# A long convolution's filter transform: groups taken in pairs, second-stage products of 404 instead of 202 columns, and the first four folds split between VectorE and GpSimd

## Chip, cores and metric

The kernel runs on one core of a Trainium2 chip. The metric is the device time of one execution in microseconds (us), median over runs. All data are float32.

## What is computed

The reference is a gated long convolution followed by a small mixture-of-experts step. What matters here is the first part, above all the filter:

```
h_mlp  = max(pos_emb @ w1, 0) @ w2          # 12608 x 128
h_filt = h_mlp * exp(-0.01 * pos)
u      = x * v                               # 4 x 12608 x 128
y      = irfft(rfft(u, 2S) * rfft(h_filt, 2S))[:S]
out    = x * y        # then 128 rows of each batch pass through an expert network
```

The kernel replaces the long FFT by a transform of length 101 x 250, done as two matrix products (two stages). The filter is transformed once, for all 128 channels; the signal is transformed for 4 batches x 128 channels.

## The kernel before

The program has three parts on the time line. `h_hid` (L274) computes the filter in time order into the buffer `big`. `h_spec` (L354) transforms the filter and writes its spectrum to DRAM (`hd`). The loop at L1040 then takes the signal, 128 steps of four channels, through forward transform, product with the filter's spectrum and inverse transform; behind it, interleaved, come the output products and the selection for the experts. The change lies in `h_spec` alone.

`h_spec` treats the 128 channels in NG = 32 groups of four, 404 columns (4 x 101) each. Per group `g`:

- **fold** (L367 to L373): one addition and one subtraction, both with two inputs in SBUF, 101 x 504 elements each. Groups 0 to 3 are folded ahead of the loop by VectorE (L390); later ones by GpSimd, each issued by `fold(g + 4)` at the end of `fwd(g)`. There are four fold buffers (`fbo`), so the fold of `g + 4` overwrites what the first stage of `g` reads.
- **first stage** (`fwd`, L375): 16 products of 101 columns. Each float32 product has two records in the trace, so 32 at L382. An even group writes two PSUM banks (`a`), an odd group the two halves of one double bank (`c`, number 73 in the order). ScalarE copies both halves into `te` (L385); `te` has two buffers.
- **second stage** (L397 to L402): 8 products of 202 columns, two column halves `h` times two parities `e` times two row halves `w`; 16 records. They write `p` and `q`, the halves of a double PSUM bank: `c_74` for even groups, `c_72` for odd ones. They use 64 rows x 64 columns of the array, the first stage 101 rows x 63 columns.
- **combination**: ScalarE copies `q` (L404), VectorE runs four instructions (L407, L408, two at L410), all of them reading `p` in PSUM. L410 writes the buffer `ht` (two buffers), which SyncE sends to `hd` (L411).

The loop at L392 runs one group ahead in the first stage: the order on TensorE is first stage of `g + 1`, second stage of `g`, first stage of `g + 2`, second stage of `g + 1`, and so on. Engines work their instructions in program order; waits between them are put in by the framework from what each instruction reads and writes. The program order of ScalarE, VectorE and GpSimd is the order in which the lines above are written.

Of the kernel before, what the change touches and what calls it, by code (L numbers as in the profile page):

```python
# [18 lines left out]
NQ = 64  # L19
N1, N2, N3 = 101, 250, 125  # L20
# [3 lines left out]
NG = 32  # L24
# [15 lines left out]
JH = (N3 + 1) // 2  # L40
# [123 lines left out]
def hyena_moe(ctx, tc, xg, x2, pos, bw, ww, wg, mw1, mw2, fo, c1, gx, cf, ci, wm, tk, out):  # L164
    nc = tc.nc
# [9 lines left out]
    def view(t, off, shape):  # L175
        n = int(np.prod(shape[1:]))
        r = t[:shape[0], off:off + n]
        if len(shape) > 2:
            ax = "abcd"[:len(shape) - 1]
            r = r.rearrange(f"p ({' '.join(ax)}) -> p {' '.join(ax)}", **dict(zip(ax[1:], shape[2:])))  # L180
        return r

    def buf(name, k, shape):
        o, n, w = OFF[name]
        return view(arena, o + k % n * w, shape)
# [7 lines left out]
    def ps1(k, shape, name):  # L193
        return view((*bank1, *bank2[::2])[k], 0, shape)

    def ps2(k, shape, name):
        return view(bank2[k], 0, shape)
# [30 lines left out]
    fo_sb = view(arena, OFF["wx"][0] + 32 * JH, [128, 2, NQ])  # L228
# [4 lines left out]
    def rev(t):  # L233
        return t.rearrange("p (s i) -> p s i", i=N1)[:, :, ::-1]

    def nat(t):
        return t.rearrange("p (s i) -> p s i", i=N1)

    def load_u(t):
        b, g = divmod(t, NG)  # L240
        if b < B:
            for k, n in enumerate("xv"):
                nc.sync.dma_start(buf(n, t, [NP, XC]), xg[b, :, g, k])

    def stage_u(t):
        if t >= B * NG:
            return
        x, v = buf("x", t, [NP, XC]), buf("v", t, [NP, XC])
        nc.gpsimd.tensor_tensor(out=x, in0=x, in1=v, op=ALU.mult)  # L249

    def load_h(t):
        if t < B * NG:
            nc.sync.dma_start(buf("ht", t, [128, 2 * HC]), hd[:, t % NG])

    def mm2(o, lhsT, rhs, **kw):
        kw = kw or dict(start=True, stop=True)
        w = 32 if spare[0] else NQ
        for a in range(0, 128, w):
            nc.tensor.matmul(o[a:a + w], lhsT=lhsT[:, a:a + w], rhs=rhs, **kw)
# [94 lines left out]
    def h_spec():  # L354
        te = {}

        def tps(g):
            if g % 2:
                t = ps2(1, [128, 2, 512], f"htp_{g}")
                return [t[:, e, :HC] for e in range(2)]  # L360
            return [ps1(e, [128, HC], f"htp_{g}_{e}") for e in range(2)]

        def pqs(g):
            t = ps2(0 if g % 2 else 2, [128, 2, 512], f"hpq_{g}")
            return [t[:, e, :HC] for e in range(2)]

        def fold(g, eng=nc.gpsimd):  # L367
            if g >= NG:
                return
            fb[g] = view(arena, fbo[g % 4], [N1, 2, 2, 4, JH])  # L370
            hg = hb[:, :, 4 * g:4 * g + 4]
            for k, op in enumerate((ALU.add, ALU.subtract)):
                eng.tensor_tensor(out=fb[g][:, k], in0=hg[:, :, :, :JH], in1=hg[:, :, :, N3:JH - 1:-1], op=op)  # L373

        def fwd(g):  # L375
            b = fb.pop(g)
            tp = tps(g)
            t = te[g] = buf("te", g, [128, 2, HC])
            for e in range(2):
                for s in range(4):  # L380
                    for w in range(2):
                        nc.tensor.matmul(tp[e][w * NQ:w * NQ + JH, s * N1:(s + 1) * N1], lhsT=b[:, w ^ e, e, s], rhs=c1_sb[:N1, 0],  # L382
                                         start=True, stop=True)
            for e in range(2):
                nc.scalar.copy(out=t[:, e], in_=tp[e])  # L385
            fold(g + 4)

        fb = {}
        for g in range(4):
            fold(g, nc.vector)  # L390
        fwd(0)
        for g in range(NG):  # L392
            if g + 1 < NG:
                fwd(g + 1)
            p, q = pqs(g)
            t = te.pop(g)
            for h in range(2):  # L397
                c = slice(h * 2 * N1, (h + 1) * 2 * N1)
                for e in range(2):
                    for w, o in enumerate((p, q)):  # L400
                        r = slice(w * NQ, w * NQ + JH)
                        nc.tensor.matmul(o[e * NQ:(e + 1) * NQ, c], lhsT=fo_sb[r, e], rhs=t[r, e, c], start=True, stop=True)  # L402
            qs = buf("qs", g, [128, HC])
            nc.scalar.copy(out=qs, in_=q)  # L404
            vs = buf("yz", g, [128, HC])
            ht = buf("sd", g, [128, 2, HC])
            nc.vector.tensor_tensor(out=nat(vs), in0=rev(p), in1=nat(qs), op=ALU.subtract)  # L407
            nc.vector.tensor_tensor(out=nat(p), in0=nat(p), in1=rev(qs), op=ALU.add)  # L408
            for e, op in enumerate((ALU.add, ALU.subtract)):
                nc.vector.tensor_tensor(out=ht[:, e], in0=p, in1=vs, op=op)  # L410
            nc.sync.dma_start(hd[:, g], ht.rearrange("p e c -> p (e c)"))  # L411
            if NG - 5 <= g < NG - 3:
                stage_u(g - NG + 5)
                load_u(g - NG + 7)
            if g == NG - 2:
                stage_u(2)
            if g >= NG - 3:
                load_h(g - NG + 3)
# [487 lines left out]
    class Experts:  # L906
# [36 lines left out]
        def second(self, yp, hs, c0, c1):  # L943
            for c in range(c0, c1):
                mm2(yp, hs[:, c], self.m2[:, c], start=(c == 0), stop=(c == 7))
# [85 lines left out]
    for t in bank2[2:] + bank1 + bank2[:2]:  # L1031
        nc.vector.memset(t, 0.0)
    h_hid()
    h_spec()
    ex = None
    te, uv, ys, sd, ph = {}, {}, {}, {}, {}
# [3 lines left out]
    for t in range(NT + LAG):  # L1040
        g = t % NG
# [3 lines left out]
        if t < NT:  # L1045
            pq = ps2(1 - t % 2, [128, 2, 512], f"pq_{t}")
# [18 lines left out]
            o = t - 1 in uv  # L1065
# [37 lines left out]
        if i >= 0 and i % NG in LA:  # L1103
            if i % NG == LA[0]:
                ph[b] = P1(b)
            k, e = divmod(LA.index(i % NG), 2)
# [60 lines left out]
```

## Time and profile before

| | |
|---|---|
| median of 3 runs | 901.03 us (898.41 to 903.42) |
| the profiled execution | 897.32 us |
| its span, first to last instruction | 895.5 us |
| mean granted TensorE clock | 0.987 |
| busy: TensorE, VectorE, GpSimd, ScalarE | 97%, 90%, 85%, 70% of the span |
| the filter transform's stage | about 33 to 116 us of the span |

The profile counts times from the first instruction of the span. "PE" is TensorE's matrix products, "PEld" its weight loads, "DVE" VectorE, "ACT" ScalarE, "POOL" GpSimd, "SP" SyncE, whose queue issues the DMAs. Ends of matrix products are modelled in the trace, starts are recorded. The idle time in brackets is that of the engine just before the instruction, with what ended it.

### The profile page before, as it was taken

The page shows a single profiled execution, that of the slowest core. Times are in us where ns is not written, and L with a number is a line of the kernel's source. Part 1 is how long each engine was busy: PE and PEld are TensorE (multiplying, and loading weights), DVE is VectorE, ACT ScalarE, POOL GpSimd, SP SyncE. Part 2 cuts the span into 40 slices and gives each one's busy share as a digit, 9 for nine tenths or more (in the row PEclk, how much of TensorE's full clock was granted, in tenths as well). Part 3 has the DMA queues.
Part 4 walks back from the last instruction along what each step waited for, and adds up shares of the span by engine and source line. Part 5 has one row for each costly group of instructions (what it writes and reads, how often), then busy time and mean ns, then how long its engine had stood idle before and what let it go on. Part 6 is the DMA issues. An engine that isn't in the chain of part 4 may idle for free.

```text
span 895.5 us, 46412 instructions
## 1 busy us (share of the span) xinstructions
PE 865.7 (97%) x19606; PEld 763.4 (85%) x19606; DVE 807.6 (90%) x1543; ACT 627.9 (70%) x2242; POOL 763.9 (85%) x834
## 2 busy tenths in 40 slices
PE   8999989999999999999999999999999999999965
PEld 6788768999999889888899798888998898879954
DVE  8998899999999899999998898999998989997883
ACT  6655575555558988885579798855698888646920
POOL 5898659999999889898999798999998989988710
PEclk9999999999999999999999999999999999999996
DMA  7044587777887967688779766788797767855810
GB/s 251 35 174 172 205 291 226 213 217 230 262 248 246 296 219 220 200 247 250 243 234 299 224 213 207 231 247 236 250 300 237 221 199 227 253 176 179 267 60 7
DMA packets 83512, 195.06 MB, mean 218 GB/s; under 512 B 9639, under 2 KB 46608, under 8 KB 83304
## 3 DMA queue, kind: packets, MB, share of 16 engines
q1 hardware_dynamic: 83048, 191.57, 67.6%
q8 instruction: 154, 2.52, 1.1%
q0 software_dynamic: 256, 0.52, 0.2%
q14 instruction: 54, 0.44, 0.2%
HBM read 151.46 MB, written 40.60 MB: 214 GB/s over the span
## 4 chain that ended last, share of the span: by engine, by line
PE 71%; DVE 16%; ACT 5%; POOL 4%; issue 3%; DMA 2%; POOLq 0%; DVEq 0%; SPq 0%; ACTq 0%
PE c L263 19%; PE a L426 15%; PE c L268 15%; ACT arena L601 4%; PE c L546 3%; PE a L542 3%; PE a L546 3%; PE c L542 3%; PE c L402 2%; PE a L382 2%; DVE arena L440 2%; DVE c L441 2%; PE c L382 2%; DVE arena L446 1%; DVE ms L696 1%
## 5 line engine op out<-in xcount | busy, mean ns | idle before, releaser
L263 PE MATMUL c<-ci_sb,arena 128*26 128x126 f32 x8128 | 261.0, 271 | 2.1 <-POOL arena L453 1.6
L263 PEld LDWEIGHTS c<-ci_sb,arena 128*26 128x26 f32 x8128 | 244.7, 104 | 5.1 <-POOL arena L453 1.8
L268 PE MATMUL c<-arena,cf_sb 128*32 128x404 f32 x2048 | 214.0, 502 | 3.3 <-ACT arena L428 1.3
L426 PE MATMUL a<-c_sb,arena 128*32 128x202 f32 (+1 forms) x4096 | 216.1, 334 | 0.0
L426 PEld LDWEIGHTS a<-c_sb,arena 128*32 128x32 f32 (+1 forms) x4096 | 174.5, 108 | 26.7 <-issue 12.8
L249 POOL TENSOR_TENSOR arena<-arena 128x500 f32<-128x500 f32 x128 | 161.9, 1265 | 11.3 <-DMA arena<-in_xg_dram 11.3
L428 ACT COPY arena<-a 128x404 f32<-128x404 f32 x256 | 128.1, 501 | 50.2 <-PE a L426 48.8
L477 ACT COPY big<-c 128x824 f32<-128x824 f32 x127 | 106.3, 837 | 78.2 <-PE c L263 77.9
L453 POOL TENSOR_TENSOR arena<-arena 128x404 f32<-128x404 f32 x127 | 124.0, 977 | 39.0 <-DVE arena L447 30.7
L601 ACT ACTIVATE arena<-arena 128x128 f32<-128x128 f32 x502 | 147.4, 299 | 11.7 <-DVE arena L591 9.5
L268 PEld LDWEIGHTS c<-arena,cf_sb 128*32 128x32 f32 x2048 | 100.8, 109 | 35.6 <-issue 18.8
L440 DVE TENSOR_TENSOR arena<-c,arena 128x808 f32<-128x808 f32 x127 | 126.8, 998 | 3.8
L441 DVE TENSOR_TENSOR c<-c,arena 128x808 f32<-128x808 f32 x127 | 126.7, 998 | 0.0
L454 POOL TENSOR_TENSOR arena<-arena 128x404 f32<-128x404 f32 x127 | 123.6, 973 | 0.0
L601 ACT ACTIVATION_READ_ACCUMULATOR arena<-arena 128x1 f32 x502 | 96.0, 191 | 0.0
L529 POOL TENSOR_TENSOR arena<-big 128x512 f32<-128x512 f32 x72 | 89.8, 1285 | 0.7 <-PE c L542 0.4
L446 DVE TENSOR_TENSOR arena<-c,arena 128x404 f32<-128x404 f32 x127 | 73.6, 579 | 12.9
L435 DVE TENSOR_TENSOR c<-c,arena 128x404 f32<-128x404 f32 x128 | 74.6, 583 | 11.6 <-ACT arena L271 8.2
L432 DVE TENSOR_TENSOR c<-c,arena 128x404 f32<-128x404 f32 x128 | 75.0, 586 | 9.6 <-ACT c L765 4.9
L497 POOL TENSOR_TENSOR big<-big,arena 128x184 f32<-128x184 f32 x128 | 74.5, 582 | 10.0
L271 ACT COPY arena<-c 128x404 f32<-128x404 f32 x128 | 63.6, 497 | 24.2 <-PE c L268 23.1
L496 POOL TENSOR_TENSOR big<-big,arena 128x184 f32<-128x184 f32 x128 | 75.0, 586 | 1.3 <-ACT arena L478 1.3
(196 smaller groups left out, 1433.5 us busy)
## 6 DMA issues: line engine op xcount, KB each, us to landing
arena<-in_xg_dram SPq DMA_DIRECT2D x256, 250.0 KB, 3.9
arena<-hd SPq DMA_DIRECT2D x128, 404.0 KB, 4.5
out_dram<-arena SPq DMA_DIRECT2D x60, 420.0 KB, 5.4
arena<-in_x_dram SPq DMA_DIRECT2D x36, 420.0 KB, 4.7
hd<-arena SPq DMA_DIRECT2D x32, 404.0 KB, 3.0
arena<-in_x_dram SPq DMA_DIRECT2D x48, 210.0 KB, 5.0
arena<-in_pos_dram SPq DMA_DIRECT2D x15, 202.0 KB, 4.5
arena<-in_x_dram SPq DMA_DIRECT2D x4, 315.0 KB, 4.5
```

The source lines that it names most:

```text
L249: nc.gpsimd.tensor_tensor(out=x, in0=x, in1=v, op=ALU.mult)
L263: nc.tensor.matmul(o[32 * k:32 * k + c.stop - c.start], lhsT=lhsT[:, c], rhs=rhs, start=True, stop=True)
L268: nc.tensor.matmul(pq[w][a:a + 32], lhsT=cf_sb[:, 2 * w + a // NQ, a % NQ:a % NQ + 32], rhs=te[:, a // NQ], start=True, stop=True)
L426: nc.tensor.matmul(tps[s // 2][c, s % 2], lhsT=u[:, s, c], rhs=c1_sb[:, 0:k + 2:k + 1], start=True, stop=True)
L428: nc.scalar.copy(out=te[:, :, 2 * h:2 * h + 2].rearrange("p e s i -> p s e i"), in_=tps[h])
L440: nc.vector.tensor_tensor(out=mt, in0=uv, in1=ht[:, 0].unsqueeze(1).to_broadcast([128, 2, HC]), op=ALU.mult)
L441: nc.vector.tensor_tensor(out=uv, in0=uv, in1=ht[:, 1].unsqueeze(1).to_broadcast([128, 2, HC]), op=ALU.mult)
L453: eng.tensor_tensor(out=nat(sd[:, 0]), in0=nat(yz[:, 0]), in1=rev(yz[:, 1]), op=ALU.add)
L454: eng.tensor_tensor(out=nat(sd[:, 1]), in0=rev(yz[:, 0]), in1=nat(yz[:, 1]), op=ALU.subtract)
L477: nc.scalar.copy(out=ay[:, t % NG, :NJ + JM, ss], in_=o3[:, :, :NJ + JM].rearrange("p s x -> p x s"))
L529: nc.gpsimd.tensor_tensor(out=cm[:, e].rearrange("p j (g s) -> p j g s", s=4), in0=av[0], in1=av[1], op=op)
L601: nc.scalar.activation(out=x, in_=x, func=AF.Copy, accum_out=self.sc[:, j:j + 1])
```

## The change

In `h_spec` the loop now works in pairs. At each even `g` it issues the first stages of `g` and `g + 1`, then the second stages of both, now as one function `second`, with four products of 404 columns in place of eight of 202. The combinations of the two groups follow as before, one per pass. Ahead of the loop groups 0 and 1 are folded by VectorE, groups 2 and 3 by GpSimd.

```
+        def second(g):
+            pq = pqs(g)
+            t = te.pop(g)
+            for e in range(2):
+                for w, o in enumerate(pq):
+                    r = slice(w * NQ, w * NQ + JH)
+                    nc.tensor.matmul(o[e * NQ:(e + 1) * NQ], lhsT=fo_sb[r, e], rhs=t[r, e], start=True, stop=True)
+            return pq
+
         fb = {}
         for g in range(4):
-            fold(g, nc.vector)
-        fwd(0)
+            fold(g, nc.gpsimd if g > 1 else nc.vector)
         for g in range(NG):
-            if g + 1 < NG:
+            if g % 2 == 0:
+                fwd(g)
                 fwd(g + 1)
-            p, q = pqs(g)
-            t = te.pop(g)
-            for h in range(2):
-                c = slice(h * 2 * N1, (h + 1) * 2 * N1)
-                for e in range(2):
-                    for w, o in enumerate((p, q)):
-                        r = slice(w * NQ, w * NQ + JH)
-                        nc.tensor.matmul(o[e * NQ:(e + 1) * NQ, c], lhsT=fo_sb[r, e], rhs=t[r, e, c], start=True, stop=True)
+                held = [second(k) for k in (g, g + 1)]
+            p, q = held[g % 2]
             qs = buf("qs", g, [128, HC])
```

How the order moves on TensorE, at the start of the stage: the difference between the two programs (a row is a run of equal instructions; L394 is the new second stage, L402 the old one).

```order
 L382 MATMUL c_73<-c_sb,arena 63x101 x16
-L402 MATMUL c_74<-arena 64x202 x8
+L394 MATMUL c_74<-arena 64x404 x4
+L394 MATMUL c_72<-arena 64x404 x4
 L382 MATMUL a_70<-c_sb,arena 63x101 x8
 L382 MATMUL a_71<-c_sb,arena 63x101 x8
-L402 MATMUL c_72<-arena 64x202 x8
 L382 MATMUL c_73<-c_sb,arena 63x101 x16
```

Both second stages now stand together behind both first stages; in every pair two changes of shape take the place of four.

The waits that these instructions carry in the changed program, for groups 2 and 3 (a name in brackets is the engine that is waited for):

```order
L382 MATMUL c_73<-c_sb,arena 63x101 x14
L394 MATMUL c_74<-arena 64x404 [waits DVE_49,Activation_49]
L394 MATMUL c_74<-arena 64x404
L394 MATMUL c_74<-arena 64x404 [waits Activation_49]
L394 MATMUL c_74<-arena 64x404
L394 MATMUL c_72<-arena 64x404 [waits DVE_49,Activation_49]
L394 MATMUL c_72<-arena 64x404
L394 MATMUL c_72<-arena 64x404 [waits Activation_49]
```

The second stage of an odd group, in `c_72`, waits for VectorE to be done with the odd group before it, and for the copies of a first stage that ended only one second stage earlier.

ScalarE in the loop, before, and then in the changed program (L404 there is L407 here):

```order
L404 COPY arena<-c_72 128x404
L385 COPY arena<-c_73 128x404 x2
L404 COPY arena<-c_74 128x404
L385 COPY arena<-a_70 128x404
L385 COPY arena<-a_71 128x404
```

```order
L385 COPY arena<-a_70 128x404
L385 COPY arena<-a_71 128x404
L385 COPY arena<-c_73 128x404 x2
L407 COPY arena<-c_74 128x404
L407 COPY arena<-c_72 128x404
```

The two copies of `q` now come one behind the other, both behind the copies of the odd group's first stage.

GpSimd ahead of the loop, in the changed program (rows 12 and on of 781): 

```order
L347 TENSOR_TENSOR big<-big,arena 101x128x4 [waits Activation_49] x14
L373 TENSOR_TENSOR arena<-big 101x504 [waits DVE_49,PE_49,Pool_49]
L373 TENSOR_TENSOR arena<-big 101x504 [waits PE_49]
L373 TENSOR_TENSOR arena<-big 101x504 x2
L373 TENSOR_TENSOR arena<-big 101x504 [waits DVE_49,PE_49]
```

Four folds stand here ahead of the first that waits for a first stage; they wait for the filter in time order to be complete, as VectorE's first fold does.

## Rows read from the trace of the kernel before

**Rows 1.** The page: busy time of TensorE and VectorE over the span, and the clock that was granted in 40 slices of it.
```profile
PE 865.7 (97%) x19606; PEld 763.4 (85%) x19606; DVE 807.6 (90%) x1543; ACT 627.9 (70%) x2242; POOL 763.9 (85%) x834
PEclk9999999999999999999999999999999999999996
```
**Rows 2.** The chain that ended last, in order of time (start, length, what), 28 to 48 us.
```profile
35.06 1.39 PE c L382 x31
36.45 0.85 PE c L402 x16
37.29 1.54 PE a L382 x32
38.83 0.84 PE c L402 x16
39.68 1.54 PE c L382 x32
41.21 0.84 PE c L402 x16
```
**Rows 3.** The time line of TensorE (start, length, line, shape, count): the start of the stage, four stages from its middle, and its end.
```profile
33.46 0.39 PE L382 MATMUL a<-c_sb,arena 101*63 101x101 f32 x4
36.38 0.92 PE L402 MATMUL c<-arena 63*64 63x202 f32 x16
...
45.91 0.92 PE L402 MATMUL c<-arena 63*64 63x202 f32 x16
46.76 1.61 PE L382 MATMUL a<-c_sb,arena 101*63 101x101 f32 x32
48.29 0.92 PE L402 MATMUL c<-arena 63*64 63x202 f32 x16
49.14 1.61 PE L382 MATMUL c<-c_sb,arena 101*63 101x101 f32 x32
50.68 0.92 PE L402 MATMUL c<-arena 63*64 63x202 f32 x16
...
109.93 0.92 PE L402 MATMUL c<-arena 63*64 63x202 f32 x16 [1.04 <-DVE arena L410]
110.78 1.58 PE L426 MATMUL a<-c_sb,arena 128*32 128x202 f32 x32
```
**Rows 4.** The same, looked at through narrow windows: the last rounds of the second stage that began at 48.29 us, the last four rounds of the first stage that began at 49.14 us, and the eight records of 404 columns on 64 x 64 of the array at L309.
```profile
48.86 0.35 PE L402 MATMUL c<-arena 63*64 63x202 f32 x4
...
50.15 0.51 PE L382 MATMUL c<-c_sb,arena 101*63 101x101 f32 x7
50.49 0.26 PE L382 MATMUL c<-c_sb,arena 101*63 101x101 f32 x2
...
10.34 0.91 PE L309 MATMUL c<-arena 64*64 64x404 f32 x8
```
**Rows 5.** The time line of ScalarE and of VectorE around the second stage of 45.91 us.
```profile
46.08 0.89 ACT L385 COPY arena<-c 128x404 f32<-128x404 f32 x2 [1.03 <-PE c L382]
46.94 0.50 ACT L404 COPY arena<-c 128x404 f32<-128x404 f32 x1
...
43.04 0.57 DVE L407 TENSOR_TENSOR arena<-c,arena 128x404 f32<-128x404 f32 x1
45.24 0.57 DVE L407 TENSOR_TENSOR arena<-c,arena 128x404 f32<-128x404 f32 x1
46.47 1.06 DVE L410 TENSOR_TENSOR arena<-c,arena 128x404 f32<-128x404 f32 x2
47.47 0.58 DVE L407 TENSOR_TENSOR arena<-c,arena 128x404 f32<-128x404 f32 x1
```
**Rows 6.** The time line of VectorE: the end of the combination of group 29, and the waits of L410 for a transfer between 48 and 112 us.
```profile
108.72 1.06 DVE L410 TENSOR_TENSOR arena<-c,arena 128x404 f32<-128x404 f32 x2
...
54.23 1.06 DVE L410 TENSOR_TENSOR arena<-c,arena 128x404 f32<-128x404 f32 x2 [0.80 <-DMA hd<-arena]
73.25 1.07 DVE L410 TENSOR_TENSOR arena<-c,arena 128x404 f32<-128x404 f32 x2 [0.75 <-DMA hd<-arena]
85.32 1.06 DVE L410 TENSOR_TENSOR arena<-c,arena 128x404 f32<-128x404 f32 x2 [0.80 <-DMA hd<-arena]
104.31 1.06 DVE L410 TENSOR_TENSOR arena<-c,arena 128x404 f32<-128x404 f32 x2 [0.73 <-DMA hd<-arena]
```
**Rows 7.** The folds at the start: time lines of VectorE and of GpSimd in narrow windows, then groups by line, VectorE's folds that started from 32.1 to 35.2 us and GpSimd's from 39.5 to 52 us (busy time, mean ns of one, idle before).
```profile
32.13 0.68 DVE L373 TENSOR_TENSOR arena<-big 101x504 f32<-101x504 f32 x1
35.70 3.01 DVE L373 TENSOR_TENSOR arena<-big 101x504 f32<-101x504 f32 x2
37.17 1.54 DVE L373 TENSOR_TENSOR arena<-big 101x504 f32<-101x504 f32 x1
...
35.20 1.51 POOL L373 TENSOR_TENSOR arena<-big 101x504 f32<-101x504 f32 x1 [3.54 <-DVE arena L373]
36.67 2.96 POOL L373 TENSOR_TENSOR arena<-big 101x504 f32<-101x504 f32 x2
...
L373 DVE TENSOR_TENSOR arena<-big 101x504 f32<-101x504 f32 x6 | 3.7, 676 | 0.1
...
L373 POOL TENSOR_TENSOR arena<-big 101x504 f32<-101x504 f32 x14 | 14.8, 1099 | 0.0
```
**Rows 8.** The chain that ended last, in order of time, 98 to 125 us: the end of the stage and the start of the signal's loop.
```profile
98.85 1.07 DVE arena L410 x2
...
99.94 4.28 DMA hd<-arena
...
109.81 5.40 DMA hd<-arena
...
115.31 1.06 DVE arena L410 x2
116.37 0.51 DVE c L435
...
120.67 1.56 PE c L268 x16
122.24 1.38 PE a L426 x31
```

## The prediction

> **What bounds the kernel now.** Start with the page: TensorE is busy for 97% of the span, at full clock almost to the end [rows 1]. So a microsecond that TensorE loses in the filter's stage is lost at the end, unless something later waits for another reason. Next the chain of waits: through the stage it runs on TensorE alone, first stage, second stage, with nothing between [rows 2]. The reader should see that no other engine appears there. The time line gives the period: second stages start at 45.91, 48.29 and 50.68 us, so a group takes 2.38 us and a pair 4.77 [rows 3].
>
> How much of this is product, how much change of shape? Within a first stage, four rounds take 50.49 - 50.15 = 0.34, 0.085 each; 16 rounds would be 1.39, and a first stage behind another first stage does take 1.39 [rows 4, 2]. Between two changes of shape it takes 1.54 [rows 2]. From the last round of a first stage (50.49) to the second stage (50.68) there pass 0.19, and from the last round of a second stage (48.86) to the next first stage (49.14) 0.28, where a round of 202 columns lasts 1.38 / 8 = 0.17 in the signal's transform [rows 3, 4, 8]. A second stage is 0.84, its four rounds would be 0.69. So changes of shape cost 0.15 + 0.15, with rounding 0.32 of the 2.38 us per group: that is what the new order can save on TensorE.
>
> Then the engines behind. VectorE needs 45.24 - 43.04 = 2.20 us per group when it is late, less than 2.38 [rows 5]. It has some 0.2 us of slack, and when it waits for a transfer it catches up. Now it can be late without TensorE noticing: the second stage of `g + 2`, which overwrites its PSUM bank, starts 4.77 us after that of `g`, while the combination is done 3.85 us after it (below). In the new order that slack decides.
>
> **The change, part by part.**
>
> *Products of 404 columns.* Half as many, twice as long. L309 has just this form on the same array tiles: eight records of 404 columns take 0.91 us from the first start to the last end, sixteen of 202 take 0.92 [rows 4, 3]. I put it at 0; the bounds are a hundredth either way per group, 0.3 us in all.
>
> *Pairs, on TensorE alone.* The changes of shape are halved: 0.32 us per pair, 4.77 - 0.32 = 4.45. If TensorE decided, 15 pairs would give 4.8 us.
>
> *Pairs, with the waits.* Count from the start T of an even second stage. ScalarE begins the copies of the odd first stage at 46.08 - 45.91 = 0.17 and ends them at 1.06; the copy of `q` runs 1.03 to 1.53; VectorE starts the combination at 47.47 - 45.91 = 1.56 [rows 5, 3]. Its four instructions end 46.47 + 1.06 - 45.24 = 2.29 later, T + 3.85. The odd group's combination follows 2.20 behind and ends at T + 6.05. The next odd second stage writes the bank that this one reads. From the end of L410 (108.72 + 1.06 = 109.78) to the product that it releases (109.93) there pass 0.15 [rows 6, 3]. So the odd second stage of the next pair cannot start before T + 6.20.
>
> From an odd second stage that had waited to the even one of the following pair TensorE has work for 110.78 - 109.93 = 0.85, a first stage with changes of shape on both sides, 1.54, and one directly behind it, 1.39: 3.78 [rows 3, 2]. Two pairs thus take 6.20 + 3.78 = 9.98, or **4.99 per pair** against 4.77 before. The copies alone would nearly do the same: the odd second stage needs both copies (T + 1.06 and a latency), so about 1.16 + 3.78 = 4.94. Both engines idle: VectorE waits for its pair, then TensorE waits for VectorE. What was covered by one group's lead in the first stage lies open now.
>
> Group 29 was combined 109.78 - 36.38 = 73.4 us after the first second stage began [rows 6, 3]. Now it is seven times 9.98 plus 6.05, 75.9: **2.5 us later**.
>
> *The folds.* VectorE ran its first six folds in 3.7 us, 0.61 each, beginning at 32.13; GpSimd was idle until 35.20. But where both fold, both slow down: VectorE's last two take 3.01, 37.17 - 35.70 = 1.47 from one to the next, GpSimd's also 36.67 - 35.20 = 1.47, against 14.8 / 14 = 1.06 later [rows 7]. 1.47 is about 0.61 + 1.06 less overlap: they take turns. So the folds that GpSimd takes over are laid upon VectorE's first two groups, which TensorE waits for. If VectorE gets the first turn, its four folds end at about 32.8, 34.3, 35.7 and 37.2, in place of 34.6 for the fourth. The second fold of group 1 goes to the second product of its first stage. Before, from the second round of the first stage of group 0 (33.46, released by the second fold) the chain was TensorE's alone. Now the first stage of group 1 proceeds at 37.26 and needs 1.39 + 0.10 to the second stage: about 38.73 against 36.38, **2.35 us later**. Bounds: 0 if the two engines did not meet, 3.3 if GpSimd gets the first turn. VectorE itself is free 1.5 us earlier, which nobody needs: its first copy of `q` now comes later still. GpSimd's later folds have time: two take 2.1 of 4.99 us for a pair.
>
> The Trainium skill (SBUF — State Buffer, "Who interferes with whom") says that a VectorE instruction with two SBUF inputs contends with a GpSimd one that reads SBUF, and that issue order decides who blocks. The 1.47 us agree. By that rule the head is 2.35 or 3.3 us according to who issues first at 32.1 us, which no row here shows; that is a rival below.
>
> *Transfers.* L410 waits for the transfer of two groups before. Usually it is in time; four times it wasn't [rows 6]. Such a one is released 104.31 - 99.92 = 4.39 us after the combination that it carries (the transfer was issued at 99.94) [rows 8, 6]. In the new order L410 comes 2 x 2.20 + 0.57 idle + 1.23 - 2.29 = 3.9 us after it: 0.46 of wait each. Before, slack of VectorE took most of it; now each passes to TensorE. I count three, **1.4 us**; the bounds are 0 and 2.8 (six). The queue of SyncE keeps its order; only the times move.
>
> *The end.* The chain there leaves by the transfer of group 29, 5.40 us, then VectorE's last L410 and the first steps of the signal's loop, and reaches TensorE at 120.67 [rows 8]. The transfers around it keep their order, so I move this whole end with group 29.
>
> **The sum.** 2.35 + 2.5 + 1.4 = 6.2 us. Against the profiled execution, 897.32, this is 903.5. That run lies 3.7 below the median of the runs, 901.03; on the median's scale the prediction is **907.2 us**, 0.7% slower.
>
> **Rivals.**
>
> 1. *The changes of shape win.* If VectorE's chain did not hold the odd second stage, a pair would take 4.45: -4.8 + 2.35 = -2.4, or 898.6. It decides where the odd bank is released by 4.45 + 0.73 (a second stage, 0.84, without the change of shape behind it, 0.11) = 5.2 us after T, not 6.20. For it: VectorE's work for a pair is only 4.4. Against: the wait stands in the program, and the chain from T to the release is built from durations that do not depend on the order. 12%; if the folds do not meet either, 896.2, another 5%.
> 2. *GpSimd folds first.* VectorE's four folds then end at about 33.8, 35.3, 36.7 and 38.2, another 0.95: 908.1. GpSimd waits for the same event as VectorE. 17%.
> 3. *The end gives back.* The 5.40 us of the transfer of group 29 come from crowding by the signal's loads; a usual late one takes 4.28 [rows 8]. Combinations are now further apart where these loads come in. If this returns 2.4 and no late transfer hits, 907.2 - 2.4 - 1.4 = 903.4. 23%. For it: the chain at the end is a transfer's, not TensorE's. Against: the loads move too.
>
> My forecast has 43%.
>
> **Range and chances.** A measurement of this kernel can tell about 0.5%, 4.5 us, from no change. The forecast and rival 2 lie beyond it: 60% slower. Rivals 1 (first form) and 3 lie within: 35%. Faster by more: 5%. The range reaches up to 907.2 + 0.95 + 1.4 + 1 (an error of 0.15 in each of seven loops) = 911 and down to 900.5, rival 3 less the loops' error and the scatter of the runs. Below it lie rival 1, 17% together, and little above.
>
> **What would show it.** Right: VectorE's four folds ahead of the loop 1.5 us apart, the first second stage at 38 to 40 us; second stages of even groups 4.9 to 5.1 us apart; each odd second stage behind an idle TensorE, released by VectorE's last combination instruction or ScalarE's copy; the eight 404-column records within 0.9 us. Wrong: even second stages 4.5 us apart with no idle time before the odd ones; folds at 0.6 us; or the stage longer as computed and the signal's loop starting no later.

## The result, and the profile after

The change is slower: 906.2 us median (905.18 to 913.08, 9 runs) against 900.5 for the kernel before, ratio 1.0084 (95% interval 1.0062 to 1.0106). The same kernel run again (`a_again`) gave 904.9 against 898.46, 1.0075 (1.0054 to 1.0096). The ratios with an interval, here and in the table below, are estimates from all runs; the two medians alone give 1.0063 and 1.0072. The forecast was 907.2 and a ratio of 1.007.

The first trace of the changed kernel comes from its longest run: 913.08 us, 7 above the median. So the second one (`a_again`, 903.3 us span) stands beside it. First the steady part, in the first trace: the time line of TensorE (start, length, line, shape, count, idle before), which answers to [rows 3].

```profile
51.00 0.91 PE L394 MATMUL c<-arena 63*64 63x404 f32 x8
52.33 0.91 PE L394 MATMUL c<-arena 63*64 63x404 f32 x8 [0.42 <-DVE arena L413]
53.17 1.61 PE L382 MATMUL a<-c_sb,arena 101*63 101x101 f32 x32
54.61 1.56 PE L382 MATMUL c<-c_sb,arena 101*63 101x101 f32 x32
56.09 0.91 PE L394 MATMUL c<-arena 63*64 63x404 f32 x8
58.07 0.91 PE L394 MATMUL c<-arena 63*64 63x404 f32 x8 [1.07 <-DVE arena L413]
58.91 1.61 PE L382 MATMUL a<-c_sb,arena 101*63 101x101 f32 x32
60.35 1.56 PE L382 MATMUL c<-c_sb,arena 101*63 101x101 f32 x32
61.84 2.01 PE L394 MATMUL c<-arena 63*64 63x404 f32 x16
```

TensorE, which did not wait in the old order, now stands idle before odd second stages, until VectorE's last combination instruction (L413, formerly L410) is done. Even second stages start at 51.00, 56.09 and 61.84: 5.09, then 5.75, against 4.77. The other half of the loop, on VectorE:

```profile
47.68 0.58 DVE L410 TENSOR_TENSOR arena<-c,arena 128x404 f32<-128x404 f32 x1 [0.97 <-ACT arena L407]
...
49.90 0.57 DVE L410 TENSOR_TENSOR arena<-c,arena 128x404 f32<-128x404 f32 x1
...
51.12 1.06 DVE L413 TENSOR_TENSOR arena<-c,arena 128x404 f32<-128x404 f32 x2
...
56.86 1.06 DVE L413 TENSOR_TENSOR arena<-c,arena 128x404 f32<-128x404 f32 x2 [0.91 <-DMA hd<-arena]
...
72.63 1.06 DVE L413 TENSOR_TENSOR arena<-c,arena 128x404 f32<-128x404 f32 x2 [0.97 <-DMA hd<-arena]
...
99.11 1.06 DVE L413 TENSOR_TENSOR arena<-c,arena 128x404 f32<-128x404 f32 x2 [1.72 <-DMA hd<-arena]
...
114.73 1.06 DVE L413 TENSOR_TENSOR arena<-c,arena 128x404 f32<-128x404 f32 x2 [0.82 <-DMA hd<-arena]
```

The even second stage of this pair began at 46.13. The combinations follow at 47.68 and 49.90 and end at 52.18, 6.05 later; the odd second stage starts at 52.33, 6.20 later: the loop of the prediction to a hundredth. VectorE waits for ScalarE's copy and then TensorE for VectorE, each in turn. Four late transfers, of the kind in [rows 6], make single steps longer: the L413 that waited 0.91 us for one starts at 56.86 and ends at 57.92, and the odd second stage follows at 58.07.

Now the start, which answers to [rows 7], in the time line of the first trace: VectorE, GpSimd, TensorE.

```profile
31.97 5.08 DVE L373 TENSOR_TENSOR arena<-big 101x504 f32<-101x504 f32 x4
...
32.04 10.19 POOL L373 TENSOR_TENSOR arena<-big 101x504 f32<-101x504 f32 x8 [0.54 <-DVE big L345]
...
34.17 1.60 PE L382 MATMUL a<-c_sb,arena 101*63 101x101 f32 x30 [0.77 <-DVE arena L373]
...
37.10 2.96 PE L382 MATMUL c<-c_sb,arena 101*63 101x101 f32 x30 [1.02 <-DVE arena L373]
39.99 2.97 PE L394 MATMUL c<-arena 63*64 63x404 f32 x16
...
46.13 2.02 PE L394 MATMUL c<-arena 63*64 63x404 f32 x16
```

The granted clock in the same trace, before, in and behind the stretch in which it was low (start and end, length, busy time and count of PE, PEld, DVE, ACT and POOL, granted clock, DMA share, GB/s):

```profile
30.00:36.70 6.70, 5.32 (x67) 4.70 (x66) 6.59 (x8) 1.91 (x5) 6.16 (x6) 1.00 0.01 2
36.80:43.50 6.70, 6.40 (x54) 4.22 (x56) 1.47 (x4) 1.86 (x4) 5.29 (x5) 0.50 0.00 0
43.60:50.00 6.40, 6.40 (x120) 4.93 (x118) 5.30 (x11) 3.53 (x8) 4.30 (x5) 1.00 0.34 133
```

The same start in the second trace, on TensorE:

```profile
34.52 1.60 PE L382 MATMUL a<-c_sb,arena 101*63 101x101 f32 x30 [0.77 <-DVE arena L373]
...
37.45 1.60 PE L382 MATMUL c<-c_sb,arena 101*63 101x101 f32 x30 [1.01 <-DVE arena L373]
38.98 1.95 PE L394 MATMUL c<-arena 63*64 63x404 f32 x16
```

VectorE's four folds take 5.08 us, where four took 2.5 before. TensorE waits 0.77 and 1.02 us for them in both traces. In the first one the granted clock was at its lower level (1.2 GHz) from 36.8 to 43.6 us, so it fell while TensorE stood in the second of these waits, and a first stage took 2.96 instead of 1.60; in the second trace it did not fall.

All kernels that were run, from their traces. "Head": VectorE's first fold to the first second stage. "Stage": from there to the end of the combination of group 29. "Steps": between even second stages, single longer ones left out (behind late transfers, behind VectorE's folds at the start, and one behind a late copy of ScalarE, see a_ht3). All in us.

| kernel | head | stage | steps | ratio to before (95%) |
|---|---|---|---|---|
| before | 4.25 | 73.4 | 4.77 | 1 |
| the change, first trace | 8.01 | 80.2 | 4.87 / 5.09 | 1.0084 (1.0062 to 1.0106) |
| a_again | 6.66 | 77.5 | 4.87 / 5.09 | 1.0075 (1.0054 to 1.0096) |
| p_only | 4.25 | 77.4 | 4.87 / 5.09 | 1.0043 (1.0015 to 1.0071) |
| f_only | 6.66 | 74.0 | 4.77 | 1.0042 (1.0027 to 1.0058) |
| p_202 | 4.25 | 78.5 | 4.88 / 5.09 | 1.0052 (1.0033 to 1.0070) |
| a_ht3 | 8.01 | 77.1 | 4.87 / 5.09 | 1.0044 (1.0021 to 1.0067) |
| a_fill | 6.69 | 77.2 | 4.87 / 5.09 | 1.0066 (1.0046 to 1.0086) |
| p_skip | 4.25 | 72.9 | 4.87 | 0.9992 (0.9974 to 1.0010) |
| b_ht3 | 4.25 | 73.0 | 4.77 | 0.9975 (0.9957 to 0.9993) |
| p_three | 4.36 | 72.2 | 4.73 | 0.9974 (0.9956 to 0.9993) |
| p_three_ht3 | 4.36 | 72.2 | 4.73 | 0.9967 (0.9953 to 0.9981) |

### The profile page after: what moved, and what is told of

Its sections match the earlier page's. It is cut to its first block, busy times and chain, and to the rows that moved or that the text cites. A ratio compares the mean times of both kernels' runs of the same rounds, so it can differ in the third digit from the quotient of the medians.

```text
span 911.3 us, 45902 instructions
## 1 busy us (share of the span) xinstructions
PE 867.8 (95%) x19350; PEld 753.7 (83%) x19350; DVE 806.7 (89%) x1539; ACT 627.6 (69%) x2242; POOL 767.6 (84%) x838
## 4 chain that ended last, share of the span: by engine, by line
PE 76%; DVE 12%; ACT 4%; DMA 3%; issue 2%; POOL 1%; POOLq 0%; DVEq 0%; ACTq 0%
PE c L263 22%; PE a L429 18%; PE c L268 18%; PE c L549 4%; ACT arena L604 3%; PE a L545 3%; PE a L549 3%; DMA hd<-arena 3%; PE c L545 3%; DVE arena L413 2%; DVE ms L699 1%; PE c L394 1%; DVE big L350 1%; PE c L382 1%; PE a L382 1%
## 5 line engine op out<-in xcount | busy, mean ns | idle before, releaser
L268 PEld LDWEIGHTS c<-arena,cf_sb 128*32 128x32 f32 x2048 | 102.0, 109 | 35.2 <-issue 18.2
L500 POOL TENSOR_TENSOR big<-big,arena 128x184 f32<-128x184 f32 x128 | 74.3, 580 | 10.0
L373 POOL TENSOR_TENSOR arena<-big 101x504 f32<-101x504 f32 x60 | 63.7, 1093 | 16.7 <-PE a L382 16.0
```

Of the source, the lines that this page charges most:

```text
L268: nc.tensor.matmul(pq[w][a:a + 32], lhsT=cf_sb[:, 2 * w + a // NQ, a % NQ:a % NQ + 32], rhs=te[:, a // NQ], start=True, stop=True)
```

## The experiments

**a_again**, no edit.

> The changed kernel once more, for a second trace. Its first trace lies 7 us above its median and shows TensorE's granted clock at its lower level from 36.8 to 43.6 us. Theory W (waits): steps between even second stages of 4.87 and 5.09 us alternate, each late transfer of hd adds about 0.9 us to one step (3 to 5 of them), the first second stage comes 38.5 to 40 us after the start, and the signal's loop begins 6 to 8 us later than in the kernel before if the clock stays high, 10 if it falls again. Theory H (head): nearly all of the loss lies ahead of the first second stage, and the steps between even second stages are 4.77 or less in the middle; the loop begins 3 us later.

Measured: head 6.66, steps of 4.87 and 5.09 with five of 5.36 to 5.67, the signal's loop 7.1 us later (121.8 against 114.7, ScalarE's first copy there). This is theory W; the head is only 2.4 of the 7.1 us. The late steps are 0.3 to 0.6 us above 5.09, not the 0.9 expected. The late transfers on VectorE, first to last:

```profile
54.15 1.06 DVE L413 TENSOR_TENSOR arena<-c,arena 128x404 f32<-128x404 f32 x2 [0.31 <-DMA hd<-arena]
...
69.52 1.06 DVE L413 TENSOR_TENSOR arena<-c,arena 128x404 f32<-128x404 f32 x2 [0.57 <-DMA hd<-arena]
...
95.37 1.06 DVE L413 TENSOR_TENSOR arena<-c,arena 128x404 f32<-128x404 f32 x2 [1.10 <-DMA hd<-arena]
...
111.00 1.06 DVE L413 TENSOR_TENSOR arena<-c,arena 128x404 f32<-128x404 f32 x2 [0.84 <-DMA hd<-arena]
```

**p_only** and **f_only**: one half of the change each.

```
p_only, in the changed kernel:
-            fold(g, nc.gpsimd if g > 1 else nc.vector)
+            fold(g, nc.vector)
f_only, in the kernel before:
-            fold(g, nc.vector)
+            fold(g, nc.gpsimd if g > 1 else nc.vector)
```

> Pairs and 404 columns as in the change, but all first four folds on VectorE as before. Theory W: first second stage at 36.4 us as before, steps of 4.99 on average plus 0.9 per late transfer, the signal's loop begins 2.5 us plus 3 to 4 late transfers, so 4 to 6 us later than before; 904 to 907 beside a before of 900.5. Theory H: the loop begins no later than before, time within 1 us of before.

> The order of before with 202 columns, only groups 2 and 3 folded by GpSimd. Theory W: VectorE's four folds last 5.1 us, the first second stage comes 2.2 us later (3.6 if the clock falls), periods stay 2.38, the loop begins 2.2 to 4 us later; 902.5 to 904.5. Theory H (the head is all of the loss): 5 to 6 us later, 906. If the head is given back downstream: as before.

Measured: p_only has the old head and the long steps, its combination of group 29 comes 4.0 us later; f_only has the long head, 2.4 us more, and the old steps. Ratios 1.0043 and 1.0042; together 1.0085, the whole change within the intervals. Neither half is given back. In the traces they are not quite independent: in p_only the second step is 5.85 us against 5.11 in a_again, because VectorE's eight folds last until about 38.5 us and the first combination starts 2.3 us after the first second stage (36.18) instead of 1.5. The other half of the change takes these 0.74 us away. For f_only the time moved by more (0.42% of 898.5, 3.8 us) than the trace's head (2.4) and stage (0.6) explain; its interval reaches down to 2.4.

The folds of f_only, on TensorE (the wait for VectorE's folds is there without any pairs):

```profile
36.36 1.60 PE L382 MATMUL a<-c_sb,arena 101*63 101x101 f32 x30 [0.78 <-DVE arena L373]
...
39.28 1.60 PE L382 MATMUL c<-c_sb,arena 101*63 101x101 f32 x30 [1.02 <-DVE arena L373]
40.81 0.92 PE L402 MATMUL c<-arena 63*64 63x202 f32 x16
```

**p_202**: p_only with the second stage in 202 columns.

```
+            for h in range(2):
+                c = slice(h * 2 * N1, (h + 1) * 2 * N1)
...
+                        nc.tensor.matmul(o[e * NQ:(e + 1) * NQ, c], lhsT=fo_sb[r, e], rhs=t[r, e, c], start=True, stop=True)
```

> As p_only, but the second stage as eight products of 202 columns. If columns cost nothing either way (theory W and the prediction): same steps and time as p_only within 0.3 us in the stage. If fewer, longer products are what gains: a pair is 0.2 us or more longer than in p_only, 3 us in all.

Measured: steps 4.88 and 5.09, as in p_only to 0.01. The column count costs and gives nothing that the steps show. Its stage is 1.1 us longer by the late transfers of its one trace (four waits of 0.55 to 1.06 us up to group 29, two of 0.75 and 0.85 in p_only); with other late transfers in each trace, the expected 0.3 us for the whole stage could not be held.

**a_ht3** and **b_ht3**: a third buffer for the combined spectrum, in the changed kernel and in the one before.

```
-            ht = buf("sd", g, [128, 2, HC])
+            ht = buf(("sd", "sd", "mt")[g % 3], g % 3, [128, 2, HC])
```

> The change, with a third buffer for the combined spectrum (mt, idle in this stage), so that the combination of a group waits for the transfer of three groups before. Theory W (late transfers pass to TensorE in the paired order, 0.3 to 1.7 us each): no step above 5.15, steps 4.87 and 5.09 alternate, the combination of group 29 ends 75.9 us after the first second stage (77.5 in a_again), the signal's loop begins 3 to 5 us later than in the kernel before, 901 to 903 beside 898.5. Theory N (the late transfers only show a delay that comes from elsewhere): the same long steps, released by another engine, and no change of time from the changed kernel, 905.

> The kernel before with the same third buffer. Theory W: VectorE has slack in the old order, so the middle of the stage stays at 4.77 per pair; only the end, where the combinations of groups 30 and 31 wait 1.7 and 0.5 us for transfers, gets shorter: the loop begins up to 2 us earlier, 896.5 to 898.5. Theory N: nothing moves.

Measured: in a_ht3 no wait for a transfer is left and the steps alternate (TensorE, then VectorE and ScalarE):

```profile
68.42 0.91 PE L394 MATMUL c<-arena 63*64 63x404 f32 x8
69.53 0.91 PE L394 MATMUL c<-arena 63*64 63x404 f32 x8 [0.20 <-ACT arena L385]
...
73.29 0.91 PE L394 MATMUL c<-arena 63*64 63x404 f32 x8
74.61 0.91 PE L394 MATMUL c<-arena 63*64 63x404 f32 x8 [0.41 <-DVE arena L413]
...
78.38 0.91 PE L394 MATMUL c<-arena 63*64 63x404 f32 x8
```

```profile
68.32 1.06 DVE L413 TENSOR_TENSOR arena<-c,arena 128x404 f32<-128x404 f32 x2
...
73.41 1.06 DVE L413 TENSOR_TENSOR arena<-c,arena 128x404 f32<-128x404 f32 x2
...
68.59 0.50 ACT L385 COPY arena<-c 128x404 f32<-128x404 f32 x1 [0.89 <-PE c L382]
```

The bracket of the short wait names ScalarE's copy, that of the long one VectorE. But the first product of an odd second stage needs only the first of ScalarE's two copies, and that ended at 69.09 (in p_skip below it starts while the second copy still runs). VectorE's L413 ends at 69.38 and at 74.47, and the odd second stages follow at 69.53 and 74.61, about 0.15 us behind it both times. So VectorE's loop sets what two steps take together, 9.96 us; ScalarE's copies only set the least that one step can be, 4.87 (p_skip).

The stage of a_ht3 is 77.1; the clock fell in this trace too and made the first step 6.17 instead of 4.8, so 75.7 without that, against the 75.9 of the prediction. One step of 5.37 is left, where ScalarE's copy of `q` starts 0.3 us late. The same copy, that of group 18, is 0.3 us late in the kernel before too (1.31 us after the start of its second stage instead of 1.03), so this comes from neither half of the change; the reason was not found.

In b_ht3 the middle does not move (4.77) and the end shortens, as expected: VectorE's last combinations come without a wait, their end 77.5 us after the first second stage instead of 80.0. Of these 2.5 us little shows in the signal's loop: its first copy comes 77.8 us after the first second stage, 78.3 before. Where the rest of the gain in time arose, the traces do not show.

```profile
111.11 0.58 DVE L407 TENSOR_TENSOR arena<-c,arena 128x404 f32<-128x404 f32 x1
...
112.35 1.06 DVE L410 TENSOR_TENSOR arena<-c,arena 128x404 f32<-128x404 f32 x2
...
114.55 1.06 DVE L410 TENSOR_TENSOR arena<-c,arena 128x404 f32<-128x404 f32 x2
```

So late transfers cost the paired order time in its middle, and the old order little before its end (in f_only a wait of 0.97 us lengthens one step by 0.17). b_ht3 is faster than the kernel before by 0.25%.

**p_three** and **p_three_ht3**: the wait for the odd bank taken away by other banks, with p_only's folds, without and with the third buffer.

```
         def tps(g):
-            if g % 2:
-                t = ps2(1, [128, 2, 512], f"htp_{g}")
-                return [t[:, e, :HC] for e in range(2)]
             return [ps1(e, [128, HC], f"htp_{g}_{e}") for e in range(2)]
         def pqs(g):
-            t = ps2(0 if g % 2 else 2, [128, 2, 512], f"hpq_{g}")
+            t = ps2(2 * g % 3, [128, 2, 512], f"hpq_{g}")
```

> Pairs and 404 columns, folds on VectorE, and the wait for the odd bank taken away by other buffers: all first stages in the two single banks, second stages in the three double banks in turn, so that a second stage waits for the combination of three groups before. Theory W: with that the changes of shape are all that is left, a pair takes 4.45 to 4.6 (the second first stage of a pair waits some 0.1 us for its banks' copies) instead of 4.98; 14 steps save 5 to 7 us against p_only, so 896 to 898, below the kernel before by 1 to 3 if late transfers leave it. If it is not the bank but the pairing itself that costs (waits for copies, order of the combinations): steps stay at 4.9 or more, 902.

> p_three with the third buffer for the combined spectrum. Theory W: no long steps, a pair 4.45 to 4.6 throughout, VectorE nearly always busy; the loop begins 4 to 6 us earlier than in the kernel before, 893 to 895 beside 898.5. If the stage's gain is given back in the signal's loop: a shorter stage and a time within 1 us of b_ht3.

Measured: both ahead of the kernel before, 0.9974 and 0.9967, but with steps of 4.73, not 4.45 to 4.6:

```profile
59.71 1.61 PE L391 MATMUL c<-arena 63*64 63x404 f32 x16
61.24 3.26 PE L379 MATMUL a<-c_sb,arena 101*63 101x101 f32 x64
64.44 1.61 PE L391 MATMUL c<-arena 63*64 63x404 f32 x16
65.97 3.26 PE L379 MATMUL a<-c_sb,arena 101*63 101x101 f32 x64
69.16 1.61 PE L391 MATMUL c<-arena 63*64 63x404 f32 x16
```

Two second stages one behind the other take 1.53, less than 2 x 0.84, and no odd one waits any more: the changes of shape are saved. But the two first stages in the same banks take 3.20 instead of 1.54 + 1.39 = 2.93: 0.27 for the copies out of these banks (the first one ends at 62.75, the second first stage starts at 62.90), where I had put 0.1. So the theory holds that the bank's release made the long steps, and my size for the price of doing without it was wrong. The gain against before, 0.3%, is 1.2 us in the stage and some more at its end: the signal's first copy comes 78.3 us after the first second stage before, 76.3 here in both. That the third buffer adds anything on top (0.9974 and 0.9967) is within the intervals.

**p_skip**: p_only with the third buffer, and one of VectorE's four instructions per group left out, so `p` lacks the addition of `q`.

```
-            nc.vector.tensor_tensor(out=nat(p), in0=nat(p), in1=rev(qs), op=ALU.add)
```

> Pairs and 404 columns, folds on VectorE, three buffers for the combined spectrum, and the addition of q to p (L411) left out, so that VectorE's chain per group is three instructions (1.6 us) in place of four (2.2). Theory W: VectorE now releases the odd bank some 5.0 us after the even second stage, before ScalarE's copies of the odd first stage are in, so the alternation of 4.87 and 5.09 goes and every step is 4.87, the copies' limit; TensorE's own 4.45 is not reached. If VectorE's chain was not what held the longer steps: 4.87 and 5.09 as before; if the copies do not hold the shorter ones: steps of 4.5.

Measured: every step but the first is 4.87. The alternation is gone, which the third buffer alone does not do (a_ht3), so VectorE's chain made the 5.09. Below it lie ScalarE's copies, and TensorE's own 4.45 is not reached: around the second stages of 60.80, whose odd one starts at 61.53, ScalarE's copies run from 60.97 to 61.87, and in the odd one the weight loads (PEld) of its second half wait for the second copy.

```profile
60.80 2.01 PE L394 MATMUL c<-arena 63*64 63x404 f32 x16
...
65.67 2.01 PE L394 MATMUL c<-arena 63*64 63x404 f32 x16
...
70.54 2.01 PE L394 MATMUL c<-arena 63*64 63x404 f32 x16
...
60.97 0.90 ACT L385 COPY arena<-c 128x404 f32<-128x404 f32 x2 [0.89 <-PE c L382]
...
61.52 0.20 PEld L394 LDWEIGHTS c<-arena 63*64 63x64 f32 x4 [0.51 <-ACT arena L385]
61.92 0.20 PEld L394 LDWEIGHTS c<-arena 63*64 63x64 f32 x4 [0.20 <-ACT arena L385]
```

**a_fill**: the change, with TensorE kept busy between the first two first stages.

```
                 fwd(g)
+                if g == 0:
+                    wp = ps2(2, [N1, N1], "fill")
+                    for _ in range(7):
+                        nc.tensor.matmul(wp, lhsT=c1_sb[:N1, 0], rhs=c1_sb[:N1, 0], start=True, stop=True)
                 fwd(g + 1)
```

> The change, with seven products that nobody reads (101 x 101 columns, as in the warm-up) between the first stages of groups 0 and 1, where TensorE otherwise waits for VectorE's and GpSimd's folds. Theory C (the idle time there lets the granted clock fall in some executions, which costs about 3 us): the clock stays at its upper level over the stage, the first second stage comes 6.7 to 7 us after VectorE's first fold, the first pair takes 4.8 to 4.9; the time is 1 to 2 below a_again's, 903 to 904, if the fall is common, the same if it is rare. If the clock fell for another reason: it falls here as well, 8 us and 6.2.

Measured: head 6.69, first pair 4.81, clock at its upper level over the whole stage; the time is that of a_again (905.3 and 904.9, ratios 1.0066 and 1.0075). The fall showed in two of the four traces with this head (the first, a_ht3; not in a_again, f_only). That the idle time lets it fall fits, but one trace without a fall does not show it, and the medians say that it is not what the change costs. Open.

## Why the prediction was right, step by step

- **Products of 404 columns, 0.** Right: 0.91 us for eight records, and p_202 has p_only's steps. The Trainium skill (TensorEngine Tiling (Array Packing), "Instruction Overhead") gives each product about 60 cycles of its own; at the granted 2.4 GHz, as an estimate, four fewer products would be 0.1 us per group. The runs do not show it: a second stage and the change of shape behind it take 0.84 us in either form [rows 2] (52.33 to 53.17 above).
- **Pairs with their waits, 4.99 per pair, 2.5 us.** Right: 4.87 and 5.09, 9.96 for two pairs against 9.98; 75.7 us in a_ht3 (the fall of the clock taken off) against 75.9, with a first step of only 4.80 and one late copy of ScalarE, 0.3 us, that nearly cancel. What I said of the copies alone, 4.94, was off: the odd second stage does not need both to start, and p_skip shows 4.87. Two such steps are 9.74, less than 9.96: VectorE's loop holds the sum, as forecast, and the copies only limit how it is split.
- **The folds, 2.35.** Right: 2.41 in a_again and f_only. VectorE began at 31.97, GpSimd at 32.04, so VectorE had the first turn and rival 2 did not come about; folds then end 1.47 us apart. That VectorE is free earlier "nobody needs" was not quite so: p_only's second step shows 0.74 us for it.
- **Late transfers, 1.4.** Right in sum for a_again (77.5 - 75.9 = 1.6). In the first trace it was 80.2 - 75.9 - 1.3 for the slow first step = 3.0, beyond the bound of 2.8. The term was mis-sized in detail: I counted three at 0.46 us each, there were four, with waits of 0.31 to 1.72. I had reckoned with the mean step of 4.99; in front of a step of 4.87, or where the transfer itself is later (5.09 us at 93.9 in the first trace), more is left.
- **The end moves with group 29.** Right: in a_again group 29 and the signal's ninth copy are both 4.1 us later, counted from the first second stage; nothing was given back (rival 3).
- **Rival 1** needed that VectorE's chain does not hold the odd second stage. It does hold it, and even without it the steps are 4.87 (p_skip) and 4.73 (p_three), not 4.45.
- **Not foreseen:** the fall of the clock. Where it came, the head took 1.35 us more and the first step 1.34 more, 2.7 in all. I had read full clock [rows 1] and did not ask what the new idle times might do to it.

The sum was 6.2; a_again has 2.4 + 4.1 = 6.5 in its trace and 6.7 us in the time (0.75% of 898.5). The head and the pairs came out by their mechanism; that the whole agrees with a_again to 0.5 us is in part luck, for late transfers alone moved it by 1.4 us between the two traces. The rest of the first trace's excess arose later, in the signal's loop, which the change does not touch: from its ninth copy to the end it took 751.8 us, in the other traces 744.2 to 748.9. What delayed it there was not looked into.

## What to carry to other kernels

Putting like stages side by side saves changes of shape only if no wait takes their place: before pairing, follow the loop from one stage's start over the engine that empties its PSUM bank back to the next writer of that bank, and divide by the steps in it. Work moved to an idle engine is free only if it does not slow what stays: folds on both engines took 1.47 us each here, while GpSimd's folds beside VectorE's combinations took 1.06 [rows 7]. Look in the trace for a place where both already run that operation. The cheapest gain lay elsewhere: a third buffer in a part of SBUF that is idle in this stage took late transfers off VectorE, and 0.25% off the kernel before.

## What the runs showed of the hardware that was not expected

- Two engines on the same kind of fold took turns, nearly for whole instructions: 1.47 us from one to the next on each, against 0.61 for VectorE and 1.06 for GpSimd alone [rows 7]. The Trainium skill (SBUF — State Buffer, "Who interferes with whom") says that issue order decides which of the two blocks. The trace agrees: VectorE started 0.07 us earlier, and its first fold took 0.68 us as before while GpSimd's took 1.54. From one to the next it is 0.2 us less than both alone together (1.67), so a little of the two overlaps.
- The granted clock fell to 1.2 GHz for 6.8 us while TensorE stood in the second of two waits, 0.77 and 1.02 us long (ended at 34.17 and 37.10 in the first trace), in two traces (the first and a_ht3) and not in two others with the same waits (a_again, f_only). In the kernel before, the wait of 1.04 us ahead of 109.93 [rows 3] had no such fall.
- Some transfers of `hd` take 4 to 5.1 us instead of a median of 2.4 to 3.0. In both traces of the changed kernel they hold up the same four groups before 30 (5, 11, 21 and 27), by different amounts; in other kernels they are partly others (6, 14, 19 and 27 before). They often go with a packet of 16 KB on an instruction queue that starts within 2.5 us of the transfer's issue: so for 25 of 28 transfers of 4 us and more, and for 73 of 183 shorter ones (all traces, issued up to 112 us, landing recorded). That this packet is the cause was not tested.
